# Low parts of most of the first MoE's weights made on the tensor engine, loads without zero rows, and tile shapes counted in the schedule

## The chip, the cores and the metric

The kernel runs on one core of one Trainium2 chip, as one program. Its engines work from queues of their own: PE (TensorE, matrix products), DVE (VectorE), ACT (ScalarE), POOL (GpSimd) and SP (SyncE, which here issues every DMA). The metric is the time of one execution on the device, in microseconds (us). Before the change it is 1143.57 us, the median of three runs (1138.99 to 1143.61).

## The reference, cut to what matters

Three layers follow each other: a recurrent attention over 768 steps (4 batches, 8 heads of 40 dimensions), and two feed-forward layers ("MoE"), each with weights of 320 x 2048 and 2048 x 320.

```python
for t in range(S):                       # attention; state is (4, 8, 40, 40)
    y[:, :, t] = einsum('bhd,bhde->bhe', rt, state)
    Sa = einsum('bhde,bhe->bhd', state, at)
    state = state * wt[:, :, None, :] - einsum('bhd,bhe->bhde', Sa, bt) \
            + einsum('bhd,bhe->bhde', vt, kt)
h = x @ w_in                             # first MoE, x is (3072, 320)
g = where(h > 0, h, exp(minimum(h, 0)) - 1)
x = g @ w_out
h = x @ w_in2                            # second MoE
out = maximum(0.01 * h, h) @ w_out2
```

Weights arrive as 64-bit floats; the output is 32-bit.

## The kernel before, in words

**Split products.** A product in full precision is made of several cheaper ones: every operand is kept as a high part (type F32R) and a low part, the rest. `x @ w` is then high*high + high*low + low*high. A matmul with F32R operands is the F32R form; one with plain 32-bit operands is the plain form. The attention uses the plain form on small tiles.

**Weights of a MoE.** `Moe.load` makes them in eight rounds, f = 0 to 7. A round has five or six tiles of 128 partitions (`parts`): two of w_in ("in", 128 x 256), in every other round one that holds the last 64 rows for two rounds ("tail", 64 + 64 rows), two of w_out ("out", 128 x 256) and one of its last columns ("ends", 128 x 128). `Moe.f32` turns each from 64-bit to 32-bit: a DMA brings the raw halves into a staging tile (e, raw, xr), ACT writes the magnitude into a work tile (wf, S or Y), and four more element-wise steps, nearly all on DVE, put the bits together there. `load` then makes the high part (a copy to `wina`, `wra` or `wouta`, on ACT or DVE) and the low part (`p.sub`: work tile minus high part, on DVE or POOL). The same code makes the second MoE's weights (`winb`, `wrb`, `woutb`): half of them are converted during the attention and parked in DRAM (`convert`, `load_f32`), the rest at the end.

**Attention.** Twelve chunks of 64 steps, each for two halves u of the batch and heads. `Attn.pre` loads W, AQ and KB and scales them; its buffers have 2 x 64 rows, of which 2 x 40 hold data and 2 x 24 are zero. `solve` is a chain of 31 pairs of small DVE instructions (tmp, TX) per chunk. `post`, `load` (V, RD, VU) and `seq` do the rest, with many small plain-form matmuls into the three shared PSUM tiles `ps`, and end in the chunk's output, which goes through DRAM to the MoE.

**MoE chunks.** Twelve chunks of 256 tokens per MoE. For each pair of 128 columns: 16 matmuls `ph<-xs,wina/wra` (8 per 128 columns), the activation into e (ACT and DVE), its split into gh and gl (DVE, ACT), and 16 matmuls `po<-gh/gl,wouta`. In the second MoE they are `ph<-xs,winb/wrb` and `ps<-woutb,gh/gl`. The first MoE runs interleaved with the attention, chunk by chunk behind it; the second comes after, when the attention's buffers have been given up ("late" pool).

**What sets the order.** `Program` records every operation with its possible engines, an assumed duration and a priority (`prio`), and `schedule` plays them through once on the host: of all operations that could start first it takes the one with the smallest priority number. Each engine's instructions are then issued in the order found, and stay in it. The priorities are a table (KEYS, in units of T per attention chunk) and lines such as `CB + CS * f` for round f of the first MoE's weights, `LB * T + LS * f` for the second's. `SWITCH` is the time that the planner adds where a plain-form group meets another group on PE. All operations are issued from one line of the helper (L403), so in the profile groups are told apart by their tiles.

Of the kernel before, what the change touches and what calls it, by code (L numbers as in the profile page):

```python
# [43 lines left out]
class View:  # L44
# [43 lines left out]
    @property  # L88
    def row(s):
        return int(s.idx.flat[0]) // (s.buf.root.size // s.buf.root.shape[0])  # L90
# [21 lines left out]
class Op:  # L112
    def __init__(s, prio, ways):
        s.prio, s.ways = prio, ways
        s.deps, s.bufs, s.next, s.wait, s.end = set(), [], [], 0, 0.0
        s.cols, s.rel, s.fp32, s.rows = 0.0, 0.0, False, {}


SLACK = dict(gpsimd=59.482, scalar=402.561, vector=1.0)
# [6 lines left out]
SWITCH = 88.0  # L126
# [4 lines left out]
MIX, DENSE = 1.42, 262.0  # L131


class Program:
# [86 lines left out]
    def mm(s, out, lhsT, rhs, start, stop, ns):  # L221
        o = s.call([("tensor", "matmul", ns)], out, lhsT, rhs, start=start, stop=stop)
        o.fp32 = lhsT.buf.group.dtype != F32R
        o.cols += rhs.n * lhsT.idx.shape[0] / 16 * (1 if lhsT.buf.group.dtype == F32R else 4) * min(1.0, -(-lhsT.n // 32) / 4)

    def tp(s, out, in_, ident):
        o = s.call([("tensor", "transpose", 89.0)], out, in_, ident)
        o.fp32 = True
        o.cols += P * 2

    def dma(s, out, in_, nbytes, rate=360.0):
# [33 lines left out]
    def schedule(s):  # L265
# [23 lines left out]
        s.ticks, order, xfer, fp32, rows = {}, [], 0.0, False, {}  # L289
        while avail:  # L290
            best, first = None, 1e30
            for o in avail.values():
# [31 lines left out]
                for w in ways:  # L324
# [5 lines left out]
                    pr = o.prio  # L330
                    if w[0] == "tensor" and o.cols > 2 * w[1]:
# [21 lines left out]
            elif e == "tensor":  # L353
                t[e] = o.end = s.pe_time(st, ns + (SWITCH if o.fp32 or fp32 else 0.0), o.cols)
                fp32 = o.fp32
# [67 lines left out]
class Moe:  # L423
# [8 lines left out]
    def __init__(s, p, w_in, w_out, tag, stacked, stage, early=0):  # L432
        s.p, s.w_in, s.w_out, s.stacked = p, w_in, w_out, stacked
# [44 lines left out]
    def load(s, prio, first=0):  # L478

        p = s.p  # L480
        for f in range(first, NF // 2):
            p.prio = prio(f)
            for kind, k, c, t in s.parts(f):
                if kind == "in":
                    hi = s.win[:, 2 * k, c]
                    p.copy(hi, t)
                    p.sub(s.win[:, 2 * k + 1, c], t, hi.bitcast(F32))
                elif kind == "tail":
                    a, b = [s.wr[:, z] for z in c]
                    p.copy(a[0:64], t[0:64])  # L490
                    p.sub(a[64:128], t[0:64], a[0:64].bitcast(F32), "v")
                    p.copy(b[0:64], t[64:128], "a")
                    p.copy(b[64:128], t[64:128])
                    p.sub(b[64:128], t[64:128], b[64:128].bitcast(F32))
                elif kind == "out":
# [3 lines left out]
                    p.sub(o[:, l : l + 2 * P], t, o[:, 0 : 2 * P].bitcast(F32))  # L499
                else:  # L500
# [3 lines left out]
                    p.sub(o[:, :, l : l + 64], t, o[:, :, 2 * P : D].bitcast(F32))  # L504
# [160 lines left out]
class Attn:  # L665
# [10 lines left out]
    def __init__(s, p, xk, xr, vt, key):  # L676
# [7 lines left out]
        g(G("memset", 100), s.mask, 1.0)  # L684
        for x in range(2):
# [30 lines left out]
    def pre(s, c, u):  # L716
# [9 lines left out]
        for x in range(2):  # L726
            r = slice(x * 64, x * 64 + 64)
            p.dma(AQ[r, x].rearrange("p h t -> p (h t)"), s.xk[c, u, r, L : L + H * C], 131e3)
        KB = p.tile("VU" if (c, u) == (0, 1) else "KB")
        p.dma(KB.rearrange("p h s t -> p (h s t)"), s.xk[c, u, :, 0:L], 524e3)  # L730
# [125 lines left out]
    def load(s, c, u):  # L856
# [9 lines left out]
        for x in range(2):  # L866
            r = slice(x * 64, x * 64 + 64)
            o = slice(64 - x * 64, 128 - x * 64)
            p.dma(RD[o], s.xr[c, u, r, 0], 131e3)
            p.dma(VU[o, :, 1 - x], s.xr[c, u, r, 1], 131e3)  # L870
# [81 lines left out]
CB, CS = 6.142, 2.266  # L952
MO, MS, MJ = 1.417, 1.006, 1.075

NV = 4
VB, VS, LB, LS = 3.032, 1.488, 12.33, 1.653

RELD = 26687.597

# [4 lines left out]
    [-50.348, -61.142, -42.2, -40.0, -42.238, -21.337, -19.972, -19.134, 24.972],  # L964
    [-46.875, -29.548, -49.555, -23.276, -35.432, 16.344, 8.636, 12.3, 3.143],
# [8 lines left out]
def rwkv_moe_kernel(tc, xk, xr, vt, sq, sv, w_in1, w_out1, w_in2, w_out2, out):  # L974
# [21 lines left out]
    for n, sh, k in (  # L996
        ("idf", [P, P], 1), ("ck", [P, 4 * NCH + 1], 1), ("mask", [P, C], 1), ("sgn", [P, 2], 1),
# [5 lines left out]
        g(n, sh, F32, k, "early", n not in ("Y", "GH"))  # L1003
# [14 lines left out]
    m1 = Moe(p, w_in1, w_out1, "a", True, ((RAW1, FLT1), (RAW2, FLT2)), NA)  # L1018
# [166 lines left out]
```

## Time and profile before

| | |
|---|---|
| median of three runs | 1143.57 us |
| the profiled execution | 1141.0 us, of it 1139.2 us between first and last instruction |
| granted TensorE clock, mean | 0.962 |
| PE busy | 1023.0 us (90%) |
| DVE busy | 837.4 us (74%) |
| ACT busy | 562.6 us (49%) |
| POOL busy | 157.0 us (14%) |
| bytes moved by DMA | 111.40 MB |

The page cuts the span into 40 slices of 28.5 us and gives the busy share of each engine in tenths. A busy PE is one that has a matmul in flight; two matmuls in flight overlap, so the start-to-start distance of matmuls, not their length, tells how fast PE goes. Durations of neighbouring DVE instructions overlap a little too. DMAs show no landing time here; a late one is seen by who waits for it.

### The profile page before, as it was taken

To read this page: it belongs to the slowest core of one execution; us is meant where nothing else is said; L and a number is where in the kernel's file an instruction comes from. 1 tells how busy PE (TensorE), PEld (TensorE's weight loads), DVE (VectorE), ACT (ScalarE), POOL (GpSimd) and SP (SyncE) were. 2 spreads that over 40 slices of the span, in tenths; PEclk is the share of its full clock that TensorE was granted. 3 is DMA by queue.
4 is the path that set the end of the run, shared out by engine and by line. 5 is a ranking of instruction groups with operands and counts; after the bars stand their busy time and mean duration, and the time that the engine had idled before them with its cause. 6 is when DMAs were issued, how large, how long until landed. Compare 5 with 4: busy or idle time off the path is not lost.

```text
span 1139.2 us, 37489 instructions
## 1 busy us (share of the span) xinstructions
PE 1023.0 (90%) x15746; PEld 979.2 (86%) x15746; DVE 837.4 (74%) x2110; ACT 562.6 (49%) x1188; POOL 157.0 (14%) x239
## 2 busy tenths in 40 slices
PE   3226399999999999999999999999999999999996
PEld 3225389899989898998999989999999999999996
DVE  7999989798979898979889896599444434443432
ACT  4544547465646555656464634576333333333332
POOL 3111322121312122212131210000000000000000
PEclk9976579999999999999999999999999999999999
DMA  7854745465546464545464422453111100111000
GB/s 188 211 139 131 179 123 130 119 157 131 146 119 153 112 163 108 139 95 137 95 149 101 96 72 51 136 154 101 26 26 26 27 26 26 26 26 26 13 12 15
DMA packets 178382, 111.40 MB, mean 98 GB/s; under 512 B 127264, under 2 KB 152096, under 8 KB 178208
## 3 DMA queue, kind: packets, MB, share of 16 engines
q1 hardware_dynamic: 178208, 108.95, 38.1%
q8 instruction: 125, 2.05, 0.8%
q14 instruction: 49, 0.40, 0.1%
HBM read 88.19 MB, written 20.71 MB: 96 GB/s over the span
## 4 chain that ended last, share of the span: by engine, by line
PE 55%; DVE 19%; issue 4%; ACT 4%; DMA 4%; SPq 1%; POOL 1%; DVEq 0%; ACTq 0%; POOLq 0%
PE ps L403 25%; PE ph L403 22%; PE po L403 8%; DVE tmp L403 2%; DVE TX L403 2%; DVE e L403 2%; DVE gl L403 2%; DVE w L403 2%; SPq L403 1%; DMA N<-scr 1%; DVE T L403 1%; DVE R L403 1%; DMA scr<-TX 1%; ACT e L403 1%; DVE AQ L403 1%
## 5 line engine op out<-in xcount | busy, mean ns | idle before, releaser
L403 PE MATMUL po<-gh,wouta 128*128 128x256 f32 x960 | 204.5, 296 | 0.0
L403 ACT ACTIVATE e<-ph 128x512 f32<-128x512 f32 x192 | 114.4, 596 | 171.3 <-PE ph L403 147.5
L403 DVE TENSOR_TENSOR gl<-e,gh 128x512 fp32r<-128x512 f32 x187 | 129.9, 694 | 84.5 <-ACT gh L403 83.7
L403 PE MATMUL ph<-xs,wina 128*128 128x256 f32 x1152 | 176.9, 290 | 1.7 <-DVE e L403 1.7
L403 PE MATMUL ps<-woutb,gh 128*128 128x320 f32 x768 | 172.1, 309 | 0.4 <-ACT gh L403 0.4
L403 ACT CAST gh<-e 128x512 fp32r<-128x512 f32 x166 | 102.7, 619 | 139.4 <-DVE e L403 77.8
L403 PE MATMUL ph<-xs,winb 128*128 128x256 f32 x1152 | 168.1, 281 | 1.6 <-DVE e L403 1.6
L403 PE MATMUL po<-gl,wouta 128*128 128x256 f32 x576 | 163.7, 284 | 1.1 <-DVE gl L403 0.9
L403 PEld LDWEIGHTS po<-gh,wouta 128*128 128x128 f32 x960 | 156.2, 191 | 5.4
L403 PEld LDWEIGHTS ph<-xs,wina 128*128 128x128 f32 x1152 | 154.8, 195 | 3.9 <-DVE e L403 2.4
L403 PEld LDWEIGHTS ph<-xs,winb 128*128 128x128 f32 x1152 | 155.0, 188 | 1.8 <-DVE e L403 1.8
L403 DVE TENSOR_TENSOR e<-ph,e 128x512 f32<-128x512 f32 x96 | 66.2, 691 | 108.6 <-ACT e L403 108.4
L403 PEld LDWEIGHTS ps<-woutb,gh 128*128 128x128 f32 x768 | 123.4, 188 | 0.6 <-ACT gh L403 0.6
L403 PE MATMUL ps<-woutb,gl 128*128 128x320 f32 x384 | 118.9, 310 | 0.2 <-DVE gl L403 0.2
L403 PEld LDWEIGHTS po<-gl,wouta 128*128 128x128 f32 x576 | 110.7, 192 | 2.3 <-DVE gl L403 2.3
L403 DVE TENSOR_TENSOR tmp<-TX,N 128x126 f32<-128x126 f32 (+22 forms) x372 | 99.1, 266 | 13.2 <-DMA N<-scr 4.7
L403 DVE TENSOR_TENSOR TX<-TX,tmp 128x126 f32<-128x126 f32 (+22 forms) x372 | 97.2, 261 | 4.0
L403 DVE SCALAR_TENSOR_TENSOR e<-e,ph 128x512 f32<-128x512 f32 x96 | 65.2, 681 | 19.1 <-ACT e L403 18.7
L403 PE MATMUL ph<-xs,wra 128*128 128x256 f32 x384 | 78.6, 287 | 0.0
L403 PE MATMUL ph<-xs,wrb 128*128 128x256 f32 x384 | 77.2, 282 | 0.0
L403 PEld LDWEIGHTS ps<-woutb,gl 128*128 128x128 f32 x384 | 72.0, 188 | 0.4 <-DVE gl L403 0.4
L403 PE MATMUL ps<-idf,KB 128*128 128x128 f32 x184 | 29.7, 305 | 42.4 <-ACT wouta L403 18.0
(169 smaller groups left out, 1703.0 us busy)
## 6 DMA issues: line engine op xcount, KB each, us to landing
KB<-xk SPq DMA_DIRECT2D x23, 512.0 KB
V<-vt SPq DMA_DIRECT2D x48, 160.0 KB
AQ<-xk SPq DMA_DIRECT2D x48, 128.0 KB
N<-scr SPq DMA_DIRECT2D x24, 256.0 KB
RD<-xr SPq DMA_DIRECT2D x48, 128.0 KB
VU<-xr SPq DMA_DIRECT2D x48, 128.0 KB
W<-xk SPq DMA_DIRECT2D x23, 260.5 KB
yd<-Y SPq DMA_DIRECT2D x48, 80.0 KB
```

What stands on the lines that cost most here:

```text
L403: getattr(getattr(s.nc, e), m)(*[res(a) for a in args], **{k: res(v) for k, v in kw.items()})
```

## The change: what it does

1. In rounds 0 to 5 of the first MoE (`NPE = 6`), the low part of the "in", "out" and "ends" tiles is no longer a subtraction on DVE or POOL. PE multiplies the work tile by the identity (plain form) and adds the high part times the negated identity (`nid`, F32R form) in a `ps` tile, and ACT copies the result to the weight tile. That is 30 low parts. Rounds 6 and 7, the tails and the second MoE keep the subtraction.
2. In a "tail", where low part and high part lie in different rows, the rounded copy is made in the low part's own rows first and is then replaced, by one DVE instruction, by minus itself plus the work tile. Before, that was a subtraction in place, which could also go to POOL.
3. AQ (from chunk 2 on), KB (from chunk 1 on), RD and VU are loaded as 40 rows per half, not 64; KB by two DMAs where one was.
4. The planner now adds SWITCH wherever the tile shape on PE changes (type, rows and columns rounded up to 32, 64 or 128), and gives an operation of the shape that PE has just used a small lead (`SAME`).
5. The numbers that set the order: SLACK, MIX, DENSE, CS (first MoE's weights farther apart), MS and MJ, VS, LS (second MoE's weights farther apart), and half of KEYS.

```diff
-                    p.sub(s.win[:, 2 * k + 1, c], t, hi.bitcast(F32))
+                    s.low(f, s.win[:, 2 * k + 1, c], t, hi)
...
-                    p.sub(o[:, l : l + 2 * P], t, o[:, 0 : 2 * P].bitcast(F32))
+                    s.low(f, o[:, l : l + 2 * P], t, o[:, 0 : 2 * P])
...
+    def low(s, f, out, t, hi):
+        p = s.p
+        if f >= s.by_pe:
+            if t.row != hi.row:
+                p.copy(out, t)
+                t, hi = out.bitcast(F32), t
+                p.call([("vector", "scalar_tensor_tensor", p._ns("vector", out, [t, hi]))], out, t, -1.0, hi, ALU.mult, ALU.add)
+            else:
+                p.sub(out, t, hi.bitcast(F32), "v" if out.row != t.row else "vp")
+            return
+        ps = p.tile("ps")[:, 0 : t.n]
+        if len(t.idx.shape) > 2:
+            ps = ps.rearrange("p (i n) -> p i n", n=64)
+        with p.group_pe():
+            p.mm(ps, s.idf, t, True, False, 1.81 * t.n)
+            p.mm(ps, s.nid, hi, False, True, MMNS * t.n)
+        p.copy(out, ps, "a")
...
-            p.dma(VU[o, :, 1 - x], s.xr[c, u, r, 1], 131e3)
+            r, o = slice(x * 64, x * 64 + E), slice(64 - x * 64, 64 - x * 64 + E)
+            p.dma(RD[o], s.xr[c, u, r, 0], 82e3)
+            p.dma(VU[o, :, 1 - x], s.xr[c, u, r, 1], 82e3)
...
-                t[e] = o.end = s.pe_time(st, ns + (SWITCH if o.fp32 or fp32 else 0.0), o.cols)
+                n = sum(a != b for a, b in zip([shape] + o.shape, o.shape))
+                t[e] = o.end = s.pe_time(st, ns + SWITCH * n, o.cols)
...
-CB, CS = 6.142, 2.266
+CB, CS = 6.142, 4.065
...
-VB, VS, LB, LS = 3.032, 1.488, 12.33, 1.653
+VB, VS, LB, LS = 3.032, 1.42, 12.33, 3.015
```

**DVE, the first MoE weight tile.** Before, from the last two steps on the work tile wf (R, Z, AQ and KB are the attention's):

```order
L403 SCALAR_TENSOR_TENSOR wf<-e_115,wf 128x256
L403 TENSOR_TENSOR AQ_139<-AQ_139,R_166 64x512 x2
L403 SCALAR_TENSOR_TENSOR wf<-e_115,wf 128x256
L403 SCALAR_TENSOR_TENSOR Z<-W_163,Z 128x520
L403 TENSOR_TENSOR wina<-wf,wina 128x256
L403 TENSOR_SCALAR R_167<-Z 128x8
```

After, the same place:

```order
L408 SCALAR_TENSOR_TENSOR wf<-e_115,wf 128x256
L408 SCALAR_TENSOR_TENSOR R_168<-W_164,R_168 128x520
L408 SCALAR_TENSOR_TENSOR wf<-e_115,wf 128x256
L408 TENSOR_TENSOR AQ_141<-AQ_141,R_168 64x512 x2
L408 CAST wina<-wf 128x256
L408 TENSOR_SCALAR S_157<-S_157 128x256
L408 TENSOR_SCALAR Y<-Y 128x256
L408 SCALAR_TENSOR_TENSOR S_157<-raw_112,S_157 128x256
```

The high part (`CAST wina<-wf`) has come to DVE, the subtraction `TENSOR_TENSOR wina<-wf,wina` is gone, and the next two work tiles (S, Y) follow at once.

**PE, early in the attention's first chunk.** Before, after the third group of `AQ,KB`:

```order
L403 MATMUL ps_130<-AQ_140,KB 64x64
L403 MATMUL ps_128<-V_154,AQ_138 64x40 x16
L403 MATMUL ps_129<-V_155,AQ_139 64x40 x16
L403 MATMUL ps_130<-idf,KB 128x128 x4
L403 MATMUL ps_128<-idf,KB 128x128 x4
L403 MATMUL ps_129<-AQ_141,KB 64x64
```

After, at the same place, five low parts, each a pair of an identity and a negated-identity matmul:

```order
L408 MATMUL ps_130<-AQ_141,KB 64x64
L408 MATMUL ps_128<-wf,idf 128x256
L408 MATMUL ps_128<-wina,nid 128x256
L408 MATMUL ps_129<-S_157,idf 128x256
L408 MATMUL ps_129<-wina,nid 128x256
L408 MATMUL ps_130<-wf,idf 128x256
L408 MATMUL ps_130<-wouta,nid 128x256
L408 MATMUL ps_128<-S_158,idf 128x256
L408 MATMUL ps_128<-wouta,nid 128x256
L408 MATMUL ps_129<-Y,idf 128x128
L408 MATMUL ps_129<-wouta,nid 128x128
L408 MATMUL ps_130<-V_155,AQ_139 64x40 x16
```

`V,AQ`, which was next, now stands behind them.

**DVE, where the second MoE begins.** Before, its first activation (`e<-ph,e`) among the last of its weights (w and woutb):

```order
L403 TENSOR_SCALAR w_11458<-w_11458 128x128
L403 SCALAR_TENSOR_TENSOR w_11461<-w_11461 128x256
L403 TENSOR_SCALAR w_11458<-w_11458 128x128
L403 SCALAR_TENSOR_TENSOR w_11461<-w_11461 128x256
L403 SCALAR_TENSOR_TENSOR w_11458<-w_11458 128x128
L403 TENSOR_TENSOR xs_111<-xr,xs_111 128x3x256
L403 TENSOR_TENSOR woutb<-w_11461,woutb 128x256
L403 SCALAR_TENSOR_TENSOR w_11458<-w_11458 128x128
L403 TENSOR_TENSOR e_115<-ph_123,e_115 128x512
L403 TENSOR_TENSOR e_116<-ph_124,e_116 128x512
```

After, its first activation:

```order
L408 TENSOR_SCALAR w_11570<-w_11570 128x128
L408 TENSOR_TENSOR gl_119<-e_115,gh_117 128x512
L408 TENSOR_TENSOR woutb<-w_11569,woutb 128x256
L408 TENSOR_SCALAR w_11570<-w_11570 128x128
L408 SCALAR_TENSOR_TENSOR e_116<-e_116,ph_125 128x512
L408 SCALAR_TENSOR_TENSOR w_11570<-w_11570 128x128
L408 TENSOR_TENSOR e_115<-ph_123,e_115 128x512
L408 SCALAR_TENSOR_TENSOR w_11570<-w_11570 128x128
L408 TENSOR_SCALAR w_11571<-w_11571 128x256
L408 CAST woutb<-w_11570 128x2x64
L408 TENSOR_SCALAR w_11571<-w_11571 128x256
L408 SCALAR_TENSOR_TENSOR w_11571<-w_11571 128x256
```

It now is the 99th instruction after the attention's last `GH`, and was the 138th; weights that stood ahead of it stand behind it.

## Rows read from the trace of the kernel before

**Rows 1.** The page: span, busy time, then PE, DVE and clock by slices.

```profile
span 1139.2 us, 37489 instructions
...
PE 1023.0 (90%) x15746; PEld 979.2 (86%) x15746; DVE 837.4 (74%) x2110; ACT 562.6 (49%) x1188; POOL 157.0 (14%) x239
...
PE   3226399999999999999999999999999999999996
...
DVE  7999989798979898979889896599444434443432
...
PEclk9976579999999999999999999999999999999999
```

**Rows 2.** Four stretches: us, busy us of PE, PEld, DVE, ACT, POOL, clock, DMA.

```profile
13.00:143.00 130.00, 53.61 (x1176) 46.57 (x1176) 123.64 (x398) 64.99 (x174) 24.41 (x39) 0.76 0.66 166
143.00:724.00 581.00, 562.38 (x11453) 527.56 (x11448) 504.41 (x1328) 319.58 (x692) 119.99 (x171) 0.98 0.48 119
724.00:785.00 61.00, 59.25 (x492) 58.62 (x492) 54.20 (x141) 43.16 (x91) 4.26 (x5) 1.00 0.53 155
785.00:1139.00 354.00, 345.40 (x2629) 344.60 (x2628) 146.96 (x226) 132.03 (x227) 0.53 (x1) 0.99 0.10 25
```

**Rows 3.** Groups on DVE, first 200 us: subtractions; count, busy us, mean ns, idle.

```profile
L403 DVE TENSOR_TENSOR wouta<-wf,wouta 128x256 fp32r<-128x256 f32 x8 | 3.9, 486 | 0.0
...
L403 DVE TENSOR_TENSOR wina<-Y,wina 128x256 fp32r<-128x256 f32 x6 | 2.5, 418 | 0.0
...
L403 DVE TENSOR_TENSOR wouta<-Y,wouta 128x128 fp32r<-128x128 f32 x3 | 0.9, 285 | 0.0
```

**Rows 4.** DVE in order of time: start us, us, instruction.

```profile
56.51 0.29 DVE L403 TENSOR_TENSOR wouta<-S,wouta 128x128 fp32r<-128x128 f32 x1
56.72 0.28 DVE L403 TENSOR_TENSOR TX<-TX,tmp 128x120 f32<-128x120 f32 x1
...
60.15 0.42 DVE L403 TENSOR_TENSOR wina<-wf,wina 128x256 fp32r<-128x256 f32 x1
60.48 0.25 DVE L403 TENSOR_TENSOR TX<-TX,tmp 128x96 f32<-128x96 f32 x1
```

**Rows 5.** PE in order of time, 39 to 144 us, with the wait before each.

```profile
39.23 0.41 PE L403 MATMUL ps<-V,AQ 128*64 128x40 f32 x2 [5.98 <-DMA V<-vt]
...
66.69 1.94 PE L403 MATMUL ps<-idf,KB 128*128 128x128 f32 x8 [17.95 <-ACT wouta L403]
...
137.34 1.97 PE L403 MATMUL ps<-idf,KB 128*128 128x128 f32 x8 [11.61 <-DVE KB L403]
...
143.54 1.03 PE L403 MATMUL ph<-xs,wina 128*128 128x256 f32 x2
```

**Rows 6.** Groups on PE: plain-form matmuls of 64 columns, F32R ones of 256.

```profile
L403 PE MATMUL ph<-xs,winb 128*128 128x256 f32 x1152 | 168.1, 281 | 1.6 <-DVE e L403 1.6
...
L403 PE MATMUL ps<-GH,KBT 128*40 128x64 f32 x768 | 27.8, 228 | 0.0
```

**Rows 7.** Groups on ACT: copies out of PSUM to SBUF.

```profile
L403 ACT COPY Q<-ps 128x320 f32<-128x320 f32 x19 | 8.0, 422 | 2.3 <-PE ps L403 2.1
```

**Rows 8.** PE in order of time at two changes of tile shape.

```profile
239.86 0.39 PE L403 MATMUL po<-gh,wouta 128*128 128x256 f32 x1
240.08 0.28 PE L403 MATMUL po<-gl,wouta 128*128 128x256 f32 x1
240.20 0.40 PE L403 MATMUL po<-gh,wouta 128*128 128x256 f32 x2
...
240.80 0.28 PE L403 MATMUL po<-gl,wouta 128*128 128x256 f32 x1
241.01 1.16 PE L403 MATMUL ps<-AQ,KB 40*64 40x64 f32 x64
```

**Rows 9.** Who waited for whom: us in total, times, longest.

```profile
DVE KB L403 <- DMA KB<-xk: 8.6, 5, 3.6
```

**Rows 10.** PE where the second MoE begins.

```profile
783.42 0.98 PE L403 MATMUL ph<-xs,winb 128*128 128x256 f32 x6 [1.64 <-DVE e L403]
```

More of the change, by code (lines that the diff above doesn't have):

```diff
@@ L115, in __init__ @@
         s.deps, s.bufs, s.next, s.wait, s.end = set(), [], [], 0, 0.0
-        s.cols, s.rel, s.fp32, s.rows = 0.0, 0.0, False, {}
-SLACK = dict(gpsimd=59.482, scalar=402.561, vector=1.0)
+        s.cols, s.rel, s.rows = 0.0, 0.0, {}
+        s.shape = []
+SLACK = dict(gpsimd=91.98, scalar=419.235, vector=1.0)
 RANK = dict(gpsimd=0, scalar=1, vector=2, tensor=0, sync=0)
@@ L227, in tp, with dma @@
         o = s.call([("tensor", "transpose", 89.0)], out, in_, ident)
-        o.fp32 = True
+        o.shape.append("transpose")
         o.cols += P * 2
-    def dma(s, out, in_, nbytes, rate=360.0):
+    def dma(s, out, in_, nbytes, rate=300.0):
         s.call([("sync", "dma_start", nbytes / rate)], out, in_)
@@ L288, in schedule @@
         late_from = None if n_early else 0.0
-        s.ticks, order, xfer, fp32, rows = {}, [], 0.0, False, {}
+        s.ticks, order, xfer, shape, rows = {}, [], 0.0, None, {}
         while avail:
@@ L330, in schedule @@
                     pr = o.prio
+                    if w[0] == "tensor" and o.shape[0] == shape:
+                        pr -= SAME
                     if w[0] == "tensor" and o.cols > 2 * w[1]:
@@ L684, in __init__ @@
         g(G("memset", 100), s.mask, 1.0)
+        s.nid = p.tile("nid")
+        g([("scalar", "mul", 160)], s.nid, s.idf, -1.0)
         for x in range(2):
@@ L726, in pre @@
         for x in range(2):
-            r = slice(x * 64, x * 64 + 64)
-            p.dma(AQ[r, x].rearrange("p h t -> p (h t)"), s.xk[c, u, r, L : L + H * C], 131e3)
+            r = slice(x * 64, x * 64 + (64 if c < 2 else E))
+            p.dma(AQ[r, x].rearrange("p h t -> p (h t)"), s.xk[c, u, r, L : L + H * C], 131e3 if c < 2 else 82e3)
         KB = p.tile("VU" if (c, u) == (0, 1) else "KB")
-        p.dma(KB.rearrange("p h s t -> p (h s t)"), s.xk[c, u, :, 0:L], 524e3)
+        if c == 0:
+            p.dma(KB.rearrange("p h s t -> p (h s t)"), s.xk[c, u, :, 0:L], 524e3)
+        else:
+            for x in range(2):
+                r = slice(x * 64, x * 64 + E)
+                p.dma(KB[r].rearrange("p h s t -> p (h s t)"), s.xk[c, u, r, 0:L], 164e3)
         p.prio = s.key(c, u, 1)
@@ L1002, in rwkv_moe_kernel @@
     ):
-        g(n, sh, F32, k, "early", n not in ("Y", "GH"))
+        g(n, sh, F32R if n == "nid" else F32, k, "early", n not in ("Y", "GH"))
     g("flag", [P, 1], mybir.dt.int32, 1)
```

37 lines of the change are left out of this document (18 added, 19 removed).

## The prediction

> **What bounds the kernel now.** I read the page first, for the shape of the span [rows 1]: PE is at 20 to 30% in the first five of forty slices (with one of 60%), at 90% or more from the sixth on; DVE is at 90% in the second to fifth slice, between 70 and 90% up to the twenty-fourth, and at 40% or less in the last twelve. So there are two limits, one after the other. The stretches say it in numbers [rows 2]. From 13 to 143 us DVE is busy 123.6 of 130 us and PE 53.6, at a mean granted clock of 0.76, that is, between its two levels of 1.2 and 2.4 GHz: the start is DVE's. From 143 to 724 us PE is busy 562 of 581 us and DVE 504: both are near their limit, and neither can be called alone. From 785 us on PE is busy without a break until the last output, DVE 147 of 354: the end is PE's, and only what happens ahead of it can shift it. The timeline of PE gives the border: its first matmul of the first MoE starts at 143.5 us, and ahead of it PE sat idle for long pieces, 17.95 us in one, waiting for operands of the attention [rows 5]. So the question is how much sooner PE gets its first MoE chunk, and what of that is kept.
>
> **The start: DVE loses subtractions.** In DVE's order, counted from the built programs, 36 low parts of `wina` and `wouta` stood before, and 10 stand now; four more leave POOL. Of the 26, 21 are 128 x 256 and 5 are 128 x 128. Their mean lengths are 0.42 to 0.49 us and 0.29 us [rows 3], but DVE overlaps neighbours: from the start of one to the start of the next it is 0.33 us and 0.21 us [rows 4]. So DVE gets back between 21 x 0.33 + 5 x 0.21 = 8.0 us and 21 x 0.49 + 5 x 0.29 = 11.7 us. I take 9.5, a little nearer the distances, since they are what DVE advances by. It has no gap there that could swallow this: its idle time in the 130 us is 6.4 us [rows 2].
>
> The first MoE itself starts sooner still. Ahead of the first split of its input (`xs<-xr,xs`) DVE has 417 instructions before and 371 now, with the same 62 steps of the solve and the same four `GH`. 46 fewer at 123.64/398 = 0.31 us each are 14.3 us. But some 20 of the 46 are only put off: with CS raised, six to seven weight tiles are put together after that point. So 14.3 us is PE's head start and 9.5 us is what DVE really saves; I count the latter, because DVE has little room later, and keep the former as the far end.
>
> **What comes in for it.** Thirty pairs of matmuls on PE and thirty copies on ACT. The trace has no plain-form matmul of 256 columns that isn't a transpose. The nearest is `GH,KBT`, 64 columns: each matmul leaves two records, so 27.8 us are 384 matmuls, 0.072 us each, two side by side [rows 6]; alone that is up to 0.145 us for 64 columns, and four times that, 0.29 (if packing won nothing) to 0.58 us, is my estimate for 256. The F32R one adds 0.12 to 0.15 us [rows 6, 8], two changes of shape some 0.2 us (below). That is 0.61 to 0.93 us for each of 24, and some 0.55 us for each of the 6 of 128 columns: at most 25 us, or 33 us at the clock of 0.76. PE has 130 - 53.6 = 76 us idle there, and in its order 29 of the 30 stand ahead of the first MoE matmul. ACT's copies take at most 0.42 us each, the length of a copy of 320 columns out of PSUM [rows 7]: 12.7 us in 65 us of idle time. Both are covered, at nothing by themselves.
>
> What isn't free is the chain. The work tile (wf, S or Y) was given back when DVE had subtracted; now it is given back when PE has read it, and PE takes its matmuls in order, with the attention's among them; the next use of the tile begins on ACT and holds DVE, which is in order too. No row shows such a wait. From below it is nothing; from above each part holds DVE for its own 0.93 us, 28 us in all. Three work tiles in turn leave DVE two others to go on with, so I take a small part, 2.5 us.
>
> **The middle: tile shapes.** A change of shape costs PE about 0.1 us: into the F32R form the second matmul comes 0.22 us after the first where 0.12 is regular, and out of it 0.21 us pass where 0.12 would [rows 8]. Counted in PE's order by the planner's own shapes, there are 385 changes before and 415 now. Sixty of those belong to the 30 low parts (in the idle start); without them 355 are left. Thirty fewer at 0.1 us are 3 us, on an engine that is 97% busy there. The bounds are 0 (if PE waits for DVE instead) and 6 us. The other kinds of instruction that the new order hands from engine to engine (DVE loses 5 copies to Q and 4 splits gl, takes 5 casts gh and 3 copies VU) come out near even; I take 0.
>
> **The loads.** 48 of 128 rows of KB, AQ, RD and VU go. What is waited for among these is KB: five waits of DVE, 8.6 us together [rows 9]. In proportion to bytes 3/8 of it, 3.2 us, would be the most to win; 22 more DMAs on SP's queue, one more for each KB, delay what is issued behind them, so a loss of about as much is the other end. I take 1 us of gain.
> A rule speaks against even that. The Trainium skill ("DMA: Bandwidth & Descriptors", on why a DMA increments its semaphore by 16) says that a DMA is spread over the largest number of engines up to 16 that divides its slowest dimension: 64 or 128 rows go to 16 engines, 40 rows to 10, and four rows per engine are what 64 rows gave as well. By that rule a load of 40 rows takes as long as one of 64, the gain is 0, and the sum below would be 1132.5 us; no row of the kernel before tells them apart.
>
> **The passage to the second MoE.** Today PE waits 1.64 us there, for a ph tile that DVE's first activation gives back [rows 10]. That activation was the 138th DVE instruction after the attention's last GH and is the 99th now: this wait goes. What is late next are the weights of the last round: their last low part was the 170th instruction and is the 173rd, 3 x 54.2/141 = 1.2 us later [rows 2], while PE's cover has shrunk, from 384 to 344 first-MoE matmuls between the last attention matmul and the first of the second MoE, 4.8 us. PE makes that up by doing other matmuls ahead of the last pair; so its wait ends up between 1.64 us shorter and some 6 us longer. I take 1.5 us longer.
>
> **The sum**, against the profiled execution's 1141.0 us (1139.2 us span and 1.8 around it; 2.6 us under the median of the three runs): -9.5 + 2.5 - 3 - 1 + 1.5 = -9.5, or **1131.5 us**. I predict 1131 us.
>
> **Rivals.**
> *More of the head start is kept.* PE, at 97% from 143.5 us on, is then the limit, and all 14.3 us come through, with the 3 to 6 us of shapes: 1141.0 - 14.3 - 4.5 - 1 + 1.5 = 1122.7, say 1122 us. For it: PE's share in the second stretch. Against it: the tiles put off have to be made by a DVE that is 87% busy. Chance 0.16.
> *It is hidden.* The middle is paced by the order, not by when it began: chunk follows chunk through DVE and PE in turn, and the six or seven tiles that were put off (some 20 DVE instructions, 6 us) land where DVE has little room. What the start gave is paid back there, and 1138 to 1144, say 1140 us, comes out. For it: DVE's 504 of 581 us. Chance 0.19.
> *Slower: the low parts queue behind the attention on PE.* Before, PE stood 6.0 us for V, 18.0 us and 11.6 us for other operands [rows 5], at no cost, for nothing urgent was behind. Now low parts are, and with them a work tile, ACT and DVE. If of each of these three waits all but 4 us reach DVE, it loses 2 + 14 + 7.6 = 23.6 us, and the sum is 1141.0 - 9.5 + 23.6 - 3 - 1 + 1.5 = 1152.6 us. It decides once DVE's idle time from 13 us to PE's first MoE matmul is over 6.4 + 12 = 18 us. Against it: the planner knows that order and has put solve steps between. Chance 0.12.
> The Trainium skill gives this rival its rule ("TensorE: Matmul & The Clock Gate", part 2, step by step): matmuls stay in program order, only weight loads are pulled ahead. By it a low part cannot pass a waiting attention matmul; the trace agrees that PE stands still in such a wait, 17.95 us in one [rows 5].
>
> **Numbers.** The forecast has 0.53 (its own range 1124 to 1137 us). A change of this kernel can be told from no change from about 0.5%, 5.7 us, that is, below 1137.9 or above 1149.3 us, against 1143.57. Faster: nearly all of the forecast, 0.50, and the first rival, 0.16: 0.66. The same: 0.03 of the forecast, 0.16 of the second rival and 0.03 of the third: 0.22. Slower: 0.09 of the third and 0.03 of the second, where the put-off tiles cost more than the start gave: 0.12. The range for 8 in 10 runs from 1114 (the first rival with all 6 us of shapes and the long end of the subtractions) to 1147 us.
>
> **What would show it.** Right: PE's first MoE matmul near 130 us; DVE's idle time ahead of it not over 12 us; PE busy over 70 us by then; some 355 changes of shape outside the start; a wait of PE of about 3 us where the second MoE begins; the second MoE's chunks at the same distance as before. Wrong: low-part matmuls on PE with idle time of many us ahead of them and DVE idle with them; a first MoE matmul at 130 us but the attention's last GH no earlier than at 720 us; or KB's waits grown.

## The result, and the profile after

The changed kernel takes 1124.84 us (median of 4 runs, 1123.66 to 1126.76), the kernel before 1143.59 us in the same comparison: a ratio of 0.9847, with a 95% interval of 0.9819 to 0.9876. The forecast was 1131 us with an own range of 1124 to 1137: the result lies at that range's low end, 6 us under the forecast and 3 us over the 1122 of the first rival. The profiled execution took 1125.35 us, 15.65 less than the one before; the sum had said 9.5 less.

The page after [rows 1 before]: the span, the busy times, and the slices of PE, DVE and the granted clock.

```profile
span 1123.6 us, 37772 instructions
PE 1046.8 (93%) x15836; PEld 992.1 (88%) x15836; DVE 827.2 (74%) x2079; ACT 566.3 (50%) x1215; POOL 160.8 (14%) x244
PE   4667879999999999999999999999999999999996
DVE  8999899899999889898979885698344444444432
PEclk9856689999999999999999999999999999999999
```

PE is at 40 to 80% in the first six slices, where the low parts now stand, with a lower granted clock in the third to fifth; from the seventh slice on it is at 90% or more. The stretches, cut where PE's first matmul of the first MoE and its last one of the attention now stand [rows 2]; columns are the length, then busy us and instructions of each engine, the mean granted clock, and DMA:

```profile
13.00:133.00 120.00, 85.29 (x1310) 66.72 (x1311) 112.03 (x355) 65.77 (x184) 23.14 (x35) 0.69 0.61 152
133.00:707.00 574.00, 554.21 (x11415) 520.99 (x11417) 504.79 (x1342) 321.54 (x705) 126.63 (x179) 0.99 0.44 106
707.00:785.00 78.00, 75.11 (x601) 73.50 (x596) 68.43 (x174) 51.22 (x107) 3.21 (x5) 0.98 0.45 133
785.00:1124.00 339.00, 329.81 (x2510) 329.00 (x2509) 133.07 (x190) 124.25 (x212) 0.00 (x0) 0.99 0.09 23
```

DVE is idle for 8.0 us up to PE's first MoE matmul (6.4 before) and busy for 111.9 us (124.2), PE has 85 us of work there (54 before). The first two stretches end 10.7 and 16.0 us earlier than before; the rest is as long as it was. PE's timeline at one of the first low parts and at the border, start and length in us [rows 5]:

```profile
28.88 1.22 PE L408 MATMUL ps<-wf,idf 128*128 128x256 f32 x2
29.54 0.78 PE L408 MATMUL ps<-wina,nid 128*128 128x256 f32 x1
...
130.89 0.78 PE L408 MATMUL ps<-wina,nid 128*128 128x256 f32 x1
131.59 1.30 PE L408 MATMUL ps<-V,KBT 128*40 128x40 f32 x32
132.82 1.18 PE L408 MATMUL ph<-xs,wina 128*128 128x256 f32 x6
```

A plain-form matmul of 256 columns leaves two records, and 0.66 us pass from the first of them to the F32R one that completes the low part. The copies out of PSUM, by form (busy us, mean ns), are as short as estimated [rows 7]:

```profile
L408 ACT CAST wina<-ps 128x256 fp32r<-128x256 f32 x12 | 4.4, 364 | 1.0 <-PE ps L408 0.9
L408 ACT CAST wouta<-ps 128x256 fp32r<-128x256 f32 x12 | 4.4, 363 | 0.9 <-PE ps L408 0.9
```

DVE's waits from 13 to 133 us (total, times, longest) show no new chain; the two longest of five groups are:

```profile
DVE wf L408 <- ACT wf L408: 2.8, 2, 1.4
DVE T L408 <- ACT T L408: 0.5, 1, 0.5
```

PE's waits from 707 to 790 us, the passage to the second MoE, where one wait of 1.64 us stood [rows 10]; there are 2.8 us together now, in small pieces:

```profile
PE ps L408 <- DVE gl L408: 1.2, 2, 0.7
PE ps L408 <- ACT gh L408: 0.8, 1, 0.8
PE ph L408 <- DVE e L408: 0.4, 1, 0.4
PE po L408 <- DVE gl L408: 0.4, 1, 0.4
```

Milestones read from PE's and DVE's timelines of both traces, in us:

| | before | after | difference |
|---|---|---|---|
| first GH of the attention done | 93.9 | 95.2 | +1.3 |
| fourth GH done, the first chunk's last | 114.9 | 109.2 | -5.7 |
| first matmul of the first MoE | 143.5 | 132.8 | -10.7 |
| seventh chunk of the first MoE begins | 485.1 | 464.5 | -20.6 |
| last matmul of the attention done | 723.4 | 707.4 | -16.0 |
| last matmul done | 1130.9 | 1115.3 | -15.6 |

### The profile page after: what moved, and what is told of

Its sections match the earlier page's. It is cut to its first block, busy times and chain, and to the rows that moved or that the text cites. A ratio compares the mean times of both kernels' runs of the same rounds, so it can differ in the third digit from the quotient of the medians.

```text
span 1123.6 us, 37772 instructions
## 1 busy us (share of the span) xinstructions
PE 1046.8 (93%) x15836; PEld 992.1 (88%) x15836; DVE 827.2 (74%) x2079; ACT 566.3 (50%) x1215; POOL 160.8 (14%) x244
## 4 chain that ended last, share of the span: by engine, by line
PE 60%; DVE 25%; DMA 5%; issue 4%; ACT 3%; SPq 2%; POOL 0%; DVEq 0%; POOLq 0%; ACTq 0%
PE ps L408 26%; PE ph L408 24%; PE po L408 10%; DVE TX L408 4%; DVE tmp L408 4%; DVE e L408 2%; DVE wf L408 2%; SPq L408 2%; DVE Y L408 2%; DMA scr<-TX 1%; DVE gl L408 1%; DVE T L408 1%; DVE w L408 1%; DMA N<-scr 1%; DMA TT<-scr 1%
## 5 line engine op out<-in xcount | busy, mean ns | idle before, releaser
L408 PE MATMUL ph<-xs,wina 128*128 128x256 f32 x1152 | 174.3, 287 | 6.6 <-DVE e L408 5.7
L408 ACT CAST gh<-e 128x512 fp32r<-128x512 f32 x161 | 99.7, 619 | 113.8 <-DVE e L408 87.9
L408 DVE TENSOR_TENSOR TX<-TX,tmp 128x126 f32<-128x126 f32 (+22 forms) x372 | 100.3, 270 | 5.1
L408 ACT ACTIVATE e<-e 128x512 f32<-128x512 f32 x96 | 60.5, 631 | 2.3
```

What stands on the lines that cost most here:

```text
L408: getattr(getattr(s.nc, e), m)(*[res(a) for a in args], **{k: res(v) for k, v in kw.items()})
```

## The experiments

They are of two kinds. In seven, **the order is kept**: PE, DVE, ACT and POOL issue what the kernel named in the table issues, in the same sequence, and only the instructions of the edit differ (the planner is given the old durations). In five, **the order is planned anew**, because the edit changes what the planner sees. Ratios are to the kernel before in the same runs; the changed kernel's own is 0.9847. The milestones are those of one profiled execution each, while single executions of one kernel lie up to 12 us apart; where medians come from different comparisons, the ratios are the safer guide.

| | median us | ratio, 95% interval | first MoE matmul | last attention matmul | last matmul |
|---|---|---|---|---|---|
| e4, order of after | 1135.92 | 0.9940 (0.9918 to 0.9962) | 141.9 | 717.6 | 1125.6 |
| e5, order of before | 1137.33 | 0.9939 (0.9918 to 0.9960) | 138.7 | 717.4 | 1124.9 |
| e9, order of before | 1137.22 | 0.9970 (0.9950 to 0.9991) | 142.8 | 720.4 | 1128.2 |
| e12, order of after | 1128.38 | 0.9877 (0.9860 to 0.9893) | 133.5 | 707.5 | 1114.0 |
| e10, order of after | 1126.25 | 0.9868 (0.9840 to 0.9897) | 134.7 | 709.2 | 1117.3 |
| e3, order of after | 1141.57 | 1.0006 (0.9987 to 1.0025) | 137.3 | 726.8 | 1133.3 |
| e11, order of after | 1254.07 | 1.0993 (1.0962 to 1.1025) | 150.9 | 833.0 | 1243.8 |
| e1, planned anew | 1145.24 | 1.0018 (1.0001 to 1.0035) | 136.8 | 725.3 | 1134.0 |
| e2, planned anew | 1148.96 | 1.0059 (1.0038 to 1.0080) | 149.4 | 731.4 | 1143.2 |
| e6, planned anew | 1145.76 | 1.0046 (1.0023 to 1.0068) | 127.5 | 724.7 | 1132.9 |
| e7, planned anew | 1151.59 | 1.0099 (1.0070 to 1.0128) | 161.0 | 727.1 | 1137.1 |
| e8, planned anew | 1144.39 | 1.0045 (1.0022 to 1.0068) | 135.8 | 727.6 | 1133.7 |

**e4: 30 subtractions put back, order kept.**

```diff
+        p.call([("vector", "tensor_sub", 1.0)], out, t, hi.bitcast(F32))
         ps = p.tile("ps")[:, 0 : t.n]
```

> The changed kernel with every engine's order kept, and 30 subtractions of DVE put in between (each writes the low part that PE and ACT then make once more). Theory: 24 x 0.33 + 6 x 0.21 = 9.2 us more of DVE in the start; first matmul of the first MoE at about 142 us (132.8 in the changed kernel), and nearly all of it is still there at the end: 1132 to 1135 us. Rival A (hidden: the middle is paced by the order and takes it up): 1125 to 1128 us. If more than 9.2 us show at the end, the middle is DVE's as well.

The first matmul of the first MoE comes 9.1 us later than in the changed kernel (9.2 expected), the last matmul 10.3 us later, the medians differ by 11.1 us. PE's timeline:

```profile
140.64 1.30 PE L408 MATMUL ps<-V,KBT 128*40 128x40 f32 x32
141.87 1.44 PE L408 MATMUL ph<-xs,wina 128*128 128x256 f32 x5
```

DVE is busy for 120.8 us up to there, 8.9 more, and idle for as long as in the changed kernel (8.1 and 8.0 us), so it is DVE's work that shifts PE. At this order DVE's time in the start is the program's time: it goes through one to one, and nothing later takes it back.

**e5: the subtractions of before cut short, order kept.**

```diff
-                    p.sub(s.win[:, 2 * k + 1, c], t, hi.bitcast(F32))
+                    s.low(f, s.win[:, 2 * k + 1, c], t, hi)
...
+        if f < 6 and s.stacked:
+            i = (slice(None),) * (len(t.idx.shape) - 1) + (slice(0, 8),)
+            p.call(ways, out[i], t[i], hi[i].bitcast(F32))
...
+    p.call([("gpsimd", "memset", 1.0)], m1.win[:, 1:4:2, 0:1536].bitcast(F32), 0.0)
```

> The kernel before with every engine's order kept, and the 30 low parts of rounds 0 to 5 (27 on DVE, 3 on POOL) cut to 8 columns, the rest left at zero; two memsets on POOL from 13 us on make the zeros. It leaves out most of these low parts. Theory: 8 to 9 us of DVE go from the start, first matmul of the first MoE at about 135 us (143.5 before), end 7 to 9 us earlier, about 1135 us. Rival A (hidden): 1141 to 1143 us. What the changed kernel has beyond this, some 10 us, is then the order's.

First MoE matmul 4.9 us earlier, last matmul 6.0 us earlier, median 6 us less: fewer than the 8 to 9 expected. The expectation had taken the cut instructions as free. DVE's timeline shows what is left of one:

```profile
58.58 0.25 DVE L403 TENSOR_TENSOR tmp<-TX,N 128x96 f32<-128x96 f32 x1
58.75 0.16 DVE L403 TENSOR_TENSOR wina<-wf,wina 128x8 fp32r<-128x8 f32 x1
58.87 0.26 DVE L403 TENSOR_TENSOR TX<-TX,tmp 128x96 f32<-128x96 f32 x1
```

From its start to the next 0.12 us pass, where 0.33 did [rows 4]. 27 on DVE (22 of 256 columns, 5 of 128) then free 22 x 0.21 + 5 x 0.09 = 5.1 us, and 4.9 came. Both kept orders agree that DVE's start is paid in full at the end, e4 more cleanly: in e5 DVE's lead over the kernel before jumps from 4.9 to 7.6 us around 160 us, where the kernel before runs at a lower TensorE clock and e5 does not (see the middle, below), and falls back to 6.0 us by 630 us.

**e3, e12, e10, e9: the loads.** First the changed kernel with 64 rows everywhere, order kept:

```diff
-            r = slice(x * 64, x * 64 + (64 if c < 2 else E))
+            r = slice(x * 64, x * 64 + 64)
...
-                r = slice(x * 64, x * 64 + E)
+                r = slice(x * 64, x * 64 + 64)
...
-            r, o = slice(x * 64, x * 64 + E), slice(64 - x * 64, 64 - x * 64 + E)
+            r, o = slice(x * 64, x * 64 + 64), slice(64 - x * 64, 128 - x * 64)
```

> The changed kernel with every engine's order kept, but AQ, KB, RD and VU loaded as 64 rows per half again (KB still by two DMAs). Theory by the forecast: the loads without zero rows are worth 1 us, so 1 us more than the changed kernel's 1124.8; DVE's waits for KB go from 5.5 to at most 8.6 us together. Rival (40 rows go to fewer DMA engines and gain nothing): no difference, or a little less time. Rival (traffic as such costs the attention): 3 us more or above.

It took 1.6% more than the changed kernel, some 17 us, against an expected 1. That looked as if the loads were the whole change. But it has KB in two DMAs of 64 rows, which neither kernel has. So three more, each with the order of PE, DVE, ACT and POOL kept: the loads of the change in the kernel before (e9), KB alone by one DMA of 128 rows (e10), and all loads of before in the changed kernel (e12). The line that matters in e10, where `swap` puts the one DMA in place of the first of the two and nothing in place of the second:

```diff
                 p.dma(KB[r].rearrange("p h s t -> p (h s t)"), s.xk[c, u, r, 0:L], 164e3)
+                p.swap(*[(KB.rearrange("p h s t -> p (h s t)"), s.xk[c, u, :, 0:L])][x:])
```

> The kernel before with the order of PE, DVE, ACT and POOL kept, and AQ (from chunk 2), KB (from chunk 1), RD and VU loaded as 40 rows per half, KB by two DMAs: the loads of the change alone. After the run with 64-row loads in the changed kernel (17 us more than the changed kernel at the same order), the theory is that SP's queue counts: issuing a load of 64 rows takes SP 0.55 to 0.75 us and one of 40 rows 0.33 to 0.43 us, some 32 us less over the attention, and 45 us of it were worth 17 us there: about 12 us, 1129 to 1133 us. Rival A (the forecast's 1 us): 1141 to 1143 us. Rival B (the loads count only in an order that was planned for them): 1138 to 1141 us.

> The changed kernel with every engine's order kept, but KB brought by one DMA of 128 rows as before, not by two of 40; AQ, RD and VU stay at 40 rows. It moves 4.3 MB more (the 64-row run moved 11 MB more) and takes some 6 us less of SP's issuing (one of 128 rows 0.40 us, two of 40 rows 0.66 us). Theory (SP's issuing counts): 1121 to 1126 us, no more than the changed kernel's 1124.8. Rival (the bytes count): 4.3/11 of 17 us more, about 1131 us.

> The changed kernel with the order of PE, DVE, ACT and POOL kept, and exactly the loads of before: AQ, RD and VU as 64 rows, KB by one DMA of 128 rows. It tells which part of the 17 us of the run with 64-row loads was what: there KB came by two DMAs of 64 rows (0.63 us of SP each, 28.4 us in all), which neither kernel has. Theory 1 (those two DMAs on SP's queue, and so KB itself, were the loss): 1126 to 1130 us, the 3 us that the loads were worth in the order of before. Theory 2 (the order of the changed kernel was planned for short loads, and AQ, RD and VU are late in it): 1134 to 1141 us.

e9 gains 3 us (0.1 to 0.5%), not 12: the theory of SP's issuing falls there. e10 and e12 are by their ratios 2 and 3 us above the changed kernel, and their intervals overlap with its own. The profiled execution of e12, its fastest by 4 us, even has its last matmul 1.3 us earlier: up to 763 us DVE's instructions stand within 2.4 us of the changed kernel's, at the end of that time 0.2 us later, and then the changed kernel's clock falls for 3.4 us, from 781.8 us on, and e12's does not. So the loads of the change are worth some 3 us in either order, in that of after not told from nothing, and of e3's 17 us 13 to 15 belong to KB in two DMAs of 64 rows (e3 against e12, medians and ratios). SP's issue of one KB at the same place, in the changed kernel, e3 and e12 in turn, and then DVE's waits for KB in e3 and e12 (5.5 us in three in the changed kernel):

```profile
36.64 0.86 SPq L408 DMA_DIRECT2D KB<-xk  x2
```

```profile
38.46 1.19 SPq L408 DMA_DIRECT2D KB<-xk  x2
```

```profile
37.67 0.54 SPq L411 DMA_DIRECT2D KB<-xk  x1
```

```profile
DVE KB L408 <- DMA KB<-xk: 10.1, 7, 3.0
```

```profile
DVE KB L411 <- DMA KB<-xk: 5.0, 4, 2.7
```

The Trainium skill ("DMA: Bandwidth & Descriptors", rules for kernel authors) says not to split a transfer into two partition halves, but to use one of 128 partitions; e3 against e12 agrees, by these 13 to 15 us. At 40 rows no run shows it: e10, with one DMA of 128, is not faster than the changed kernel with two of 40.

DVE's longer waits for KB are 5 us of e3's loss. Most of the rest is in PE's clock: 28.1 us of PE's work between its first matmul of the first MoE and its last of the attention runs at the lower of the two levels, 4.8 us in e12 (table below). One place in e3: DVE waits for KB, then PE stands for 1.78 us (up to 556.48 us), and then PE works for 10.3 us at half the clock (columns as in the stretches after the change).

```profile
553.43 1.23 DVE L408 TENSOR_TENSOR KB<-KB,Z 128x1024 f32<-128x1024 f32 x1 [2.13 <-DMA KB<-xk]
```

```profile
556.90:567.20 10.30, 10.22 (x174) 9.43 (x176) 6.46 (x17) 3.22 (x7) 1.44 (x2) 0.50 0.17 44
```

Ahead of this wait DVE's instructions stand 11.8 us behind the same ones of the changed kernel, after the slow stretch 18.3 us: a wait of 2.1 us goes with a loss of 6.5.

**e11: loads that bring the same rows twice, by one DMA.** Destination 128 rows, source 2 x 64 with the first step zero.

```diff
+        src = View(in_.buf, in_.idx, in_.steps + (lambda ap: ap.unsqueeze(0).to_broadcast([2, 64, n]),))
+        s.ops[-1].ways[0][2][:] = [] if q else [("sync", "dma_start", (both, src), {})]
...
             p.dma(N[q * 64 : q * 64 + 64].rearrange("p r c -> p (r c)"), src, 262e3)
+            p.twice(q, N.rearrange("p r c -> p (r c)"), src)
```

> The changed kernel with every engine's order kept, and the loads that bring the same 64 rows twice, to both halves (N, and the last 64 rows of x in both MoEs), made by one DMA of 128 rows each that reads its source twice, where two of 64 rows were: 38 DMAs fewer. SP spends 0.70 us on each N and 0.55 us on each x tail, 0.35 to 0.40 us on one of 128 rows: 12 x 1.0 + 12 x 0.75 = 21 us less issuing up to the last attention chunk. Theory (SP's issuing counts, 17 us for 45): 5 to 8 us less, 1117 to 1120 us. Rival (these loads are not waited for): 1123 to 1126 us. Rival (a source read twice is slower to land and the solve waits for N): 1127 us or more.

129 us more than the changed kernel. The issue is as short as hoped (0.59 us for one N), but N lands late: the solve's first step waits 7.15 us where it did not wait, and DVE's waits for N are 64.2 us in all; the rest of the 129 us was not followed. SP's timeline, DVE's, and DVE's waits:

```profile
30.34 0.59 SPq L415 DMA_DIRECT2D N<-scr  x1
```

```profile
44.10 0.19 DVE L415 TENSOR_TENSOR tmp<-TX,N 128x31 f32<-128x31 f32 x1 [7.15 <-DMA N<-scr]
```

```profile
DVE tmp L415 <- DMA N<-scr: 64.2, 8, 10.0
```

Here the rule on the number of DMA engines that the prediction weighed shows itself: the slowest dimension of this source is 2, which by the Trainium skill ("DMA: Bandwidth & Descriptors", on why a DMA increments its semaphore by 16) leaves two engines. The trace agrees: from 34 to 37 us, when N alone is on its way, the 16 engines are busy for a share of 0.13 (the last but one number), which is two of them.

```profile
34.00:37.00 3.00, 0.00 (x0) 0.00 (x0) 2.81 (x9) 1.91 (x7) 1.18 (x1) 1.00 0.13 53
```

**e1, e2, e7: one half of the change without the other.** The low parts back on DVE (e1: `NPE = 0`), the low parts by PE alone in the kernel before (e2), and the change with the old numbers (e7; SWITCH and the planner's assumed DMA rate, also changed, stay).

```diff
-NPE = 6
+NPE = 0
```

> The changed kernel with all low parts back on DVE and POOL (NPE = 0); the order is planned anew with the changed numbers. Theory (the start is DVE's, and what DVE is spared there is kept): 32 subtractions of wina and wouta on DVE instead of 10, about 9 us more DVE work ahead of the attention's first GH; first matmul of the first MoE 6 to 10 us later than the changed kernel's 132.8 us; time about 1134 us. Rival A (the gain comes from the planner's rule and numbers, the low parts are hidden either way): 1123 to 1128 us. Rival B (order alone is worth half): about 1130 us.

> The kernel before with the low parts of rounds 0 to 5 by PE and nothing else of the change (its loads, its planner's rule and its numbers). Theory: DVE is spared 26 subtractions, 8 to 10 us, and the end comes that much earlier, about 1135 us; but only 8 DVE instructions fewer stand ahead of the first split of the first MoE's input (410 after 418), so PE's head start itself is only some 3 us, and if it is the head start that counts the time is 1140 us. Rival A (the numbers do it): 1143 us.

> The changed kernel with the numbers of before (KEYS, SLACK, MIX, DENSE, CS, MS, MJ, VS, LS) under the new rule for PE; low parts by PE and loads as changed. Theory, after the run in which the low parts alone made the kernel slower (1149 us): with these numbers the first MoE's rounds come close together (CS 2.266), 447 DVE instructions stand ahead of the first split (372 in the changed kernel), the low parts queue behind the attention on PE, and DVE stands: first matmul of the first MoE at 148 us or later, 1140 to 1150 us. Rival (the rule on shapes is what makes the low parts fit): 1125 to 1132 us.

Each took longer than the kernel before, e1 by a hair. For e1 and e2 no theory or rival had that; for e7 the theory had, with 1140 to 1150 us for 1151.6. In e1 the head start is there (first MoE matmul 6.7 us earlier than before), but the stretch up to the last attention matmul is 588.5 us long, where it was 579.9 before and is 574.6 after. In e2 and e7 the start itself is lost: DVE is idle for 16.0 us up to the first MoE matmul in e2 and 15.3 in e7 (6.4 before), and e7's DVE also has more work there (132.7 us, 124.2 before). The windows, e1 and then e2:

```profile
13.00:136.80 123.80, 54.20 (x1193) 46.84 (x1191) 117.35 (x378) 61.52 (x164) 25.05 (x40) 0.87 0.58 149
136.80:725.00 588.20, 562.97 (x11445) 529.38 (x11444) 508.68 (x1336) 323.82 (x707) 123.90 (x177) 0.98 0.43 104
```

```profile
13.00:149.00 136.00, 94.73 (x1496) 75.16 (x1498) 119.97 (x390) 75.58 (x209) 28.24 (x42) 0.67 0.65 166
```

What DVE waits for in e2 is hardly PE, as the third rival had it. ACT and DVE at two places next to each other:

```profile
56.55 0.43 ACT L403 ACTIVATE Y<-xr 128x256 f32<-128x256 f32 x1 [1.48 <-DMA xr<-w_in]
60.06 0.43 ACT L403 ACTIVATE wf<-e 128x256 f32<-128x256 f32 x1 [2.93 <-DMA e<-w_in]
...
57.01 0.29 DVE L403 TENSOR_SCALAR Y<-Y 128x256 f32<-128x256 f32 x1 [1.32 <-ACT Y L403]
60.52 0.29 DVE L403 TENSOR_SCALAR wf<-wf 128x256 f32<-128x256 f32 x1 [1.52 <-ACT wf L403]
```

DVE waits for ACT, and ACT for the next raw weights: with DVE spared and the rounds as close as before (CS 2.266), the next weights are not there yet. Such waits are 4.7 us of DVE's in five places; 0.6 us is put down to PE, and where ACT waits for PE to have read wf or Y (five times, 4.0 us together) no wait of DVE follows at once. The rest of the 16.0 us is spread over other waits, for ACT, POOL and DMAs. The larger CS of the change puts other work between the rounds. This is read from the trace of e2; CS alone was not tried.

**e6, e8: the rule on shapes, and all rounds by PE.**

```diff
-                n = sum(a != b for a, b in zip([shape] + o.shape, o.shape))
+                n = int(any(z == "transpose" or z[0] != F32R for z in [shape, o.shape[0]] if z))
```

> The changed kernel planned by the old rule for PE (SWITCH of 88 wherever a plain-form group meets another, no SAME lead); low parts by PE, loads and the table of numbers as changed. The order has 451 changes of tile shape, 415 in the changed kernel. Theory: 36 x 0.1 us = 3.6 us more, against a somewhat earlier start (355 DVE instructions ahead of the first split of the first MoE's input, 372 in the changed kernel): 1125 to 1130 us. Rival (the rule is what carries the middle): 1133 us or more. Rival (shapes cost nothing where PE waits anyway): 1120 to 1124 us.

> The changed kernel with the low parts of all eight rounds by PE (NPE = 8), planned anew. Ten more subtractions (3 us) leave DVE after the first MoE has begun, and ten more pairs come to PE there, 10 x 0.7 us = 7 us, with 429 changes of shape (415). Theory (PE bounds the middle): 1127 to 1133 us. Rival (the middle is DVE's): 1120 to 1123 us.

Both are above their theory, by 16 and 11 us; e6 is where its first rival put it (1133 us or more). e6 has the earliest first MoE matmul of all (127.5 us), and still the longest middle:

```profile
127.50:724.70 597.20, 568.29 (x11508) 533.59 (x11506) 509.49 (x1365) 326.66 (x717) 117.51 (x169) 0.97 0.43 104
```

36 more changes of shape at 0.1 us are 3.6 of its 22.6 us over the changed kernel's 574.6; what the others are is read next. All five orders planned anew ended at 1144 to 1152 us, whatever was edited: an edit that makes the planner start over costs some 20 us or more against this one order, and such a run doesn't price its edit. No run beat the changed kernel.

**What the middle is made of, in every order.** The middle runs from PE's first matmul of the first MoE to its last of the attention. In it the clock granted to PE falls to the lower of its two levels for some stretches. In the kernel before there are four (columns as in the stretches above; the last but two is the clock), in the changed kernel one, besides 0.5 us at its start:

```profile
143.50:148.90 5.40, 5.40 (x30) 5.20 (x24) 5.30 (x17) 5.06 (x11) 1.52 (x2) 0.50 0.62 171
155.80:162.60 6.80, 6.80 (x64) 6.29 (x68) 6.24 (x25) 1.57 (x4) 1.13 (x2) 0.50 0.40 107
217.20:220.60 3.40, 3.40 (x73) 3.18 (x72) 2.45 (x10) 0.37 (x1) 0.00 (x0) 0.50 0.11 39
329.80:333.30 3.50, 3.50 (x45) 3.21 (x45) 2.49 (x10) 0.09 (x1) 0.00 (x0) 0.51 0.08 19
```

```profile
150.30:157.20 6.90, 3.54 (x16) 3.54 (x17) 6.84 (x21) 3.86 (x8) 1.89 (x2) 0.51 0.72 167
```

What the lower level costs shows in one group of the changed kernel at either level: six matmuls last 1.44 us to the start of the next group at 153.66 us, and 0.72 us at 158.16 us.

```profile
153.66 1.65 PE L408 MATMUL ph<-xs,wina 128*128 128x256 f32 x6 [5.75 <-DVE e L408]
155.10 0.63 PE L408 MATMUL ph<-xs,wra 128*128 128x256 f32 x2
...
158.16 0.88 PE L408 MATMUL ph<-xs,wina 128*128 128x256 f32 x6
158.88 0.40 PE L408 MATMUL ph<-xs,wra 128*128 128x256 f32 x2
```

So half of the time that PE works at the lower level is my estimate of its cost. PE's middle in us, from one trace each:

| | middle | PE idle | PE busy | of it at the lower clock | busy less half of that |
|---|---|---|---|---|---|
| before | 579.9 | 18.6 | 561.3 | 19.0 | 551.8 |
| e5, order of before | 578.7 | 19.1 | 559.6 | 12.5 | 553.4 |
| e9, order of before | 577.6 | 17.4 | 560.3 | 15.5 | 552.5 |
| after | 574.6 | 19.8 | 554.8 | 3.9 | 552.8 |
| e4, order of after | 575.8 | 20.2 | 555.6 | 7.0 | 552.1 |
| e10, order of after | 574.5 | 19.5 | 555.0 | 5.3 | 552.3 |
| e12, order of after | 574.0 | 18.8 | 555.2 | 4.8 | 552.8 |
| e3, order of after | 589.5 | 22.6 | 566.9 | 28.1 | 552.9 |
| e1, planned anew | 588.5 | 25.2 | 563.3 | 24.2 | 551.2 |
| e6, planned anew | 597.3 | 28.9 | 568.4 | 31.9 | 552.4 |
| e8, planned anew | 591.8 | 24.1 | 567.7 | 22.4 | 556.5 |

By this estimate PE's work in the middle is the same within some 2 us everywhere but in e8, which has ten more low parts. (e2 and e7 are left out: their middle begins 6 and 18 us later than before, with less of the work left to it.) What differs is how much of it runs at the lower clock, and how long PE stands. The order of before has 12 to 19 us at the lower clock in three traces, that of after 4 to 7 in four (e3 with its late KB aside): half of the difference is some 5 us, which is what the whole middle gained. Of e6's 22.7 us, 14 are the clock and 9 PE's standing; nothing is left there for 36 more changes of shape. Ahead of such falls PE had stood for operands, 5.75 us in the changed kernel, 1.15 and 0.90 us shortly before 329.8 us in the kernel before; that standing PE brings the falls was not tested by itself.

## Why the prediction was right, point by point

The direction, the path (DVE's start, then PE) and the price of DVE's time were right. The number was 6 us short, and the first rival's 1122 us came nearer. Of the two terms that make the difference, the start was put too low, and the middle came out near its size for a reason that the prediction does not have.

- **The start, -9.5.** Right, and the two kept orders show it: the same DVE time is 9.1 us at the first MoE matmul in one and 4.9 (5.1 by the distances) in the other, and arrives at the end (10.3 and 6.0). The prices by distance from start to start were the right ones, nearer than the lengths.
- **The chain through PE and ACT, +2.5.** Too much: DVE's idle time grew from 6.4 to 8.0 us, 1.6, and no wait for PE or for the given-back tile is among it. Start and chain together were put at -7; PE's first MoE matmul moved by 10.7, toward the 14.3 that I had set aside as head start. This is the term that was mis-sized most, by 3.7 us. DVE's work ahead of that point fell by 12.3 us (124.2 to 111.9), the subtractions and the tiles that were put off, and its idle time took back 1.6. The tiles that were put off cost the middle nothing to be seen: the same work of PE (552 us) passed there, with 2 us more of DVE's. The first rival's mechanism, that PE is the limit from there on and all of its head start is kept, thus held here; its size of 14.3 us did not.
- **The low parts covered by PE's and ACT's idle time.** Right: 85 us of work for PE by 133 us, over 70 as forecast and 31 more than before (25 to 33 were put), and copies of 0.36 us, under the bound of 0.42.
- **Tile shapes, -3.** The middle lost 5.3 us, against 3 of the shapes and 1 of the loads, but not by the shapes: PE worked 6.5 us less, and 7.5 us is what half of 15.1 us less at the lower clock comes to. Without that its work is 1.0 us more, where 30 fewer changes at 0.1 us should have shown 3 less; e6 with 36 more shows nothing either. Changes of shape may still cost something below the 2 us that this comparison tells apart. The prediction put the clock of the middle at nothing, without a word; that the two came out alike is luck.
- **The loads, -1 (3.2 either way).** Right in size: 3 us (1 to 6) in the order of before, and in that of after some 3 us, which the intervals don't tell from nothing.
- **The passage, +1.5.** PE's waits there went from 1.64 to 2.8 us, 1.2 longer. Between the last attention matmul and the last matmul lie 407.9 us now and 407.5 before: +0.4. The second MoE's first matmul comes 21.2 us earlier (748.7 and 769.9 us), and 9.1 us of that go into its first chunk, which takes 38.4 us to the start of the second where it took 29.3.
- **The sum.** -10.7 - 5.3 + 0.4 = -15.6, which the profiled executions show, where -9.5 was forecast. e5 and e9 bring some 6 and 3 us apart from each other in the order of before, which with the 27 x 0.12 = 3 us that the 8-column pieces still cost is 12 of the 17 to 19 us of the medians. In the order of after e4 prices 30 subtractions (26 were DVE's before) at 11 us and e12 the loads at 3 or less. The rest, some 5 us, is the order's, and the clock in the middle is enough for it; which of its numbers brings that stays open.
- **The rivals.** *It is hidden* fell by e4: nothing was paid back. *Slower* did not come here, but e2 and e7 come near it (16.0 and 15.3 us of idle time of DVE, where 18 was the point from which it decides); in e2 the waits that the rows name are the weights' DMAs (4.7 us) and others, and hardly PE (0.6 us).

## What to carry to other kernels

Where an engine is busy without a break ahead of the first work of the next one, price an instruction by the distance to its neighbour's start; here it came through to the end one to one. Where PE is the limit, compare how much of its work ran at the lower clock before a difference is put down to the instructions: here a short wait went with a loss three times as long. When a planner sets the order, hold the order fixed and change the instruction alone: only such runs priced anything here, and a run that plans anew measures the planner's luck with it. Before a run that undoes a part is believed, see that it holds nothing that neither kernel had: two DMAs of 64 rows looked like the whole gain.

## What the runs showed of the hardware that was not expected

- A DVE subtraction of 8 columns still takes 0.12 us from start to start, a third of one of 256 columns (0.33 us).
- SP takes longer to issue a load of 64 rows than one of 40 or of 128: 1.19 us for two of 64, 0.86 for two of 40, 0.54 for one of 128, of the same KB; medians of one KB load over the whole run are 0.55 us for 64 rows (e3), 0.33 for 40 (after) and 0.40 for 128 (before, e12). It mattered only where the load itself was waited for.
- One DMA whose source repeats 64 rows by a first step of zero kept DVE waiting 6 to 10 us for 512 KB, eight times, with two of 16 DMA engines at work; two plain ones of half the size did not (1.9 us of waits for N in all).
- A plain-form matmul of 256 columns takes 0.66 us to the start of the next at the lower clock (48.00 us of the changed kernel) and 0.35 at the higher (41.86 us). At 28.88 us it takes 0.66 too, though the page shows no lowered clock: the trace's clock record begins at 41.1 us only (before: 70.4 us), and if the lower level held before it, the mean clock of a start, 0.69 or 0.76 [rows 2], reads too high.
- Where PE is the limit, a wait of 2.1 us for one load was followed by 10.3 us of PE's work at half the clock (e3); the program stood 6.5 us later behind it.
